# Cross network: the first layer's remainder products gathered at its end, and the last layer opened in column tiles

## The chip, the core and the metric

One core of a Trainium2 chip runs the whole computation. The core has five engines with instruction queues of their own: TensorE (PE, matrix products, with PEld for its weight loads), VectorE (DVE), ScalarE (ACT), GpSimd (POOL) and SyncE (SP, which here only issues DMAs). The metric is the device time of one launch in microseconds, smaller is better; the median of three runs stands for a kernel.

## The reference

A cross network of six layers. All arrays are bf16; B is 4096, D is 416 (26 x 16):

```python
def reference(x0, ws, bs):          # x0 [4096, 416], ws [6, 416, 416], bs [6, 416]
    x = x0
    for l in range(ws.shape[0]):
        x = x0 * (x @ ws[l] + bs[l]) + x
    return x
```

Each layer needs the whole previous one along D, but rows of the batch are independent of each other.

## The kernel before, in words

**Layout.** For the first five layers the data are transposed: D on the partitions, batch along the free dimension. 416 is 3 x 128 + 32, so there is a main part of three blocks (`XM`, index k or m) and a remainder of 32 rows (`XR`). The batch is cut into two halves `s` of 2048 columns, and each half into four column groups `g` of 512. The remainder's 32 rows of the four groups of one half are stacked on the 128 partitions of `XR`. Three buffers `XM[0..2]` and `XR[0..2]` hold x0 and, in turns, the layers' outputs. `XRd` holds x0's remainder once more, with its upper and lower 64 partitions exchanged, for the first layer's products of block m = 1.

**One tile of work.** For an output block m: products over k with `WM` (`full`, L212, in the first layer; `mm_full`, L179, with 32 output columns each and four side by side on the array, in the later ones), and products with the remainder rows `WR` (`row`, L219; `mm_row`, L185; 32 contraction rows each, four side by side). ScalarE adds the bias and moves the result from PSUM to SBUF (L163, `ew_main`), VectorE multiplies it by x0 (L164) and adds the layer's input (L167). The 32 remainder outputs are made by `mm_rem` (L191 with `WD`, a block-diagonal copy of the weights, and L196), and finished by `ew_rem` (L171 on ScalarE, L172 and L173 on VectorE).

**PSUM and t buffers.** All PSUM tiles come from one pool with four slots of two banks; a new tile waits until ScalarE has read the one that held its slot. ScalarE writes into six `t` buffers, which VectorE frees.

**First layer** (`first_layer(s)`, L206). For each half: the first two column groups of blocks 0 to 2 (`pa`), the remainder rows, then the other two groups (`pb`), their remainder rows, then `mm_rem` for this half. x0 arrives by transposed loads (`load_x0t`, eight, on SyncE's queue, one per half and group). x0's remainder arrives as 64-byte pieces: for the first half straight into `xrig` by four loads on ScalarE's queue (`load_xrem0`), for the second into `xrem` by one load on SyncE's queue, between two of the transposed ones (`load_xrem1`, L84), which GpSimd regroups into `xrig` (L132). `x0_rem(s)` turns `xrig` by four PE transposes (L155) into a PSUM tile, and VectorE copies it out three times (L158): once to `XR[0]`, twice, 64 partitions each, to `XRd`. For the second half this stands at the end of the first half's work: its four transposes follow the first half's `mm_rem`.

**Layers 1 to 4** (loop at L280). Six tiles (s, m) are worked off in pairs; n = 0, 2, 4 is the pair's first index. After the pair n = 0 comes `rem_pair` (L265), the remainder products of both halves. Layer 4's outputs go by transposed DMAs into `XLrows` (batch rows on the partitions).

**Last layer** (from L313). The roles are swapped: 128 columns of x are the weights and `WM` streams through, so that outputs have batch rows on the partitions. Eight quads of four 128-row tiles are worked off two quads at a time (`rounds`, L360). A round opens with `done` tiles through `mm_q_full` (L325), then the remainder rows and the bias (L331, L334, `mm_q_rem`), then the other tiles. ScalarE copies out (L352), VectorE multiplies by `X0rows` and adds `XLrows` (L353, L342), and a DMA writes the output.

**What sets the order.** A scheduler orders instructions on each engine by the program's order and its own estimate of when inputs are ready; `tc.keep_in_program_order` pins an instruction to the program's order on its engine. [...]

Of the kernel before, what the change touches and what calls it, by code (L numbers as in the profile page):

```python
# [9 lines left out]
ACT = mybir.ActivationFunctionType  # L10
ALU = mybir.AluOpType
BF16 = mybir.dt.bfloat16
# [4 lines left out]
def kernel(  # L17
# [43 lines left out]
    xrem = big.tile([P, 16, R], BF16)  # L61
    xrig = big.tile([P, NS, 4, P], BF16)
    XRd = big.tile([P, NS * CW], BF16)
# [9 lines left out]
    def load_x0t(s, g):  # L73
        c0 = col0(s, g)
        nc.sync.dma_start_transpose(out=XM[0][:, :, c0:c0 + CW], in_=x0[c0:c0 + CW, 0:NK * P])

    def load_xrem0():
        with nc.allow_non_contiguous_dma(reason="64B row segments"):
            for i in range(4):
                nc.scalar.dma_start(xrig[:, 0, i, :].rearrange("p (g r) -> p g r", g=NG), x0_v[:, i:16:4, NK * P:D])  # L80

    def load_xrem1():
        with nc.allow_non_contiguous_dma(reason="64B row segments"):
            nc.sync.dma_start(xrem[:], x0_v[:, 16:32, NK * P:D])  # L84

# [27 lines left out]
    load_x0t(1, 0)  # L113
    load_xrem1()
    for g in range(1, NG):
# [36 lines left out]

    def x0_rem(s, tpr):
        for i in range(4):
            nc.tensor.transpose(tpr[:, 128 * i:128 * i + 128], xrig[:, s, i, :], ident[:])  # L155
# [4 lines left out]
    def ew_main(l, s, m, h, pt, cur, nxt, pin=False):  # L160
        c0 = col0(s, 2 * h)
        t = tpool.tile([P, 2 * CW], BF16, name="t")
        nc.scalar.activation(t[:], pt[:].rearrange("p a b -> p (a b)"), ACT.Identity, bias=bM[:, m, l:l + 1], scale=1.0)  # L163
        prod = nc.vector.tensor_tensor(out=t[:], in0=t[:], in1=XM[0][:, m, c0:c0 + 2 * CW], op=ALU.mult)  # L164
        if pin:
            tc.keep_in_program_order(prod)
        nc.vector.tensor_tensor(out=nxt[:, m, c0:c0 + 2 * CW], in0=t[:], in1=cur[:, m, c0:c0 + 2 * CW], op=ALU.add)  # L167

    def ew_rem(l, s, pr, curR, nxtR):
        tr = tpool.tile([P, 2 * CW], BF16, name="t")  # L170
        nc.scalar.activation(tr[:, 0:CW], pr, ACT.Identity, bias=bR[:, l:l + 1], scale=1.0)  # L171
        nc.vector.tensor_tensor(out=tr[:, 0:CW], in0=tr[:, 0:CW], in1=XR[0][:, CW * s:CW * s + CW], op=ALU.mult)  # L172
        nc.vector.tensor_tensor(out=nxtR[:, CW * s:CW * s + CW], in0=tr[:, 0:CW], in1=curR[:, CW * s:CW * s + CW], op=ALU.add)  # L173

# [31 lines left out]
    def first_layer(s):  # L206
# [20 lines left out]
        if s == 0:  # L227
            for m in range(NK):
                full(pa[m], m, 0, 0, False)
            tp0 = psum.tile([P, CW], BF16, tag="ps", name="tpr")  # L230
            x0_rem(0, tp0[:])
# [11 lines left out]
        for m in range(NK):  # L243
            ew_main(0, s, m, 0, pa[m], cur, nxt)
        for m in range(NK):
# [34 lines left out]
    for l in range(1, LL):  # L280
# [12 lines left out]
        for n in range(0, len(tiles), 2):  # L293
# [12 lines left out]
            finish(tb)  # L306
            if n == 0:
                rem_pair(l, cur, curR, nxtR, feeds_last)
# [9 lines left out]
    def q_cols(q, g):  # L318
        s, i = quads[q]
        c = col0(s, g) + 128 * i  # L320
        return slice(c, c + 128)

    def mm_q_full(q, g, py, closes):
        for k in range(NK):
            nc.tensor.matmul(py[:, 0:D], lhsT=cur[:, k, q_cols(q, g)], rhs=WM[:, l, k, :],  # L325
                             start=((not closes) and k == 0), stop=(closes and k == NK - 1))
# [34 lines left out]
    for q, at, done in rounds:  # L361
# [49 lines left out]
```

## Time and profile before

| | us |
|---|---|
| median of three runs | 130.45 |
| lowest, highest | 130.38, 130.53 |
| the profiled execution | 130.58 |
| its span, first to last instruction | 128.8 |

| engine | busy, us | share of the span |
|---|---|---|
| PE | 123.6 | 96% |
| DVE | 106.7 | 83% |
| ACT | 86.9 | 67% |
| POOL | 6.2 | 5% |

By stage the span is cut so: the first layer up to about 26.8 us, layers 1 to 4 about 19.2 us each up to 103.7 us, the last layer from there on. TensorE's granted clock was 1.00 in every stage.

| window, us | PE busy | DVE busy | ACT busy | DMA share |
|---|---|---|---|---|
| 11.0 to 17.0 | 6.00 | 4.26 | 5.36 | 1.07 |
| 17.0 to 21.4 | 4.40 | 4.24 | 1.69 | 1.15 |
| 21.4 to 26.8 | 5.40 | 5.30 | 5.00 | 1.13 |
| 26.8 to 46.0 | 19.20 | 18.32 | 14.14 | 0.67 |
| 103.7 to 115.5 | 11.80 | 10.75 | 8.52 | 1.10 |
| 115.5 to 128.8 | 8.91 | 10.26 | 7.94 | 0.56 |

How to read it: busy time is the time in which an engine had an instruction under way; the DMA share is that of the core's 16 DMA engines and can pass 1 where packets overlap. A chain of waits is followed back from the last instruction, at each step to what released it; its lines are start, length, engine, tile and line number. In the timeline, "[0.29 <-ACT t L163]" says that the engine stood idle for 0.29 us before this instruction and that an instruction of ScalarE ended it.

### The profile page before, as it was taken

The page shows a single profiled execution, that of the slowest core. Times are in us where ns is not written, and L with a number is a line of the kernel's source. Part 1 is how long each engine was busy: PE and PEld are TensorE (multiplying, and loading weights), DVE is VectorE, ACT ScalarE, POOL GpSimd, SP SyncE. Part 2 cuts the span into 40 slices and gives each one's busy share as a digit, 9 for nine tenths or more (in the row PEclk, how much of TensorE's full clock was granted, in tenths as well). Part 3 has the DMA queues.
Part 4 walks back from the last instruction along what each step waited for, and adds up shares of the span by engine and source line. Part 5 has one row for each costly group of instructions (what it writes and reads, how often), then busy time and mean ns, then how long its engine had stood idle before and what let it go on. Part 6 is the DMA issues. An engine that isn't in the chain of part 4 may idle for free.

```text
span 128.8 us, 3973 instructions
## 1 busy us (share of the span) xinstructions
PE 123.6 (96%) x1691; PEld 55.1 (43%) x1691; DVE 106.7 (83%) x195; ACT 86.9 (67%) x99; POOL 6.2 (5%) x18
## 2 busy tenths in 40 slices
PE   7999999999999999999999999999999999999960
PEld 3343443344545444434444544444444445445420
DVE  0023989999999898989898989898989899898991
ACT  0138873887848667848668848668858896569670
POOL 4004300600000000000000000000000000000000
PEclk9999999999999999999999999999999999999999
DMA  4999999999990000000000000000297999985754
GB/s 95 244 231 207 163 153 264 253 328 333 336 291 9 5 0 8 0 0 5 0 5 0 5 0 5 0 5 0 45 163 169 119 237 191 217 261 186 235 178 138
DMA packets 42102, 16.37 MB, mean 127 GB/s; under 512 B 30906, under 2 KB 42084, under 8 KB 42084
## 3 DMA queue, kind: packets, MB, share of 16 engines
q1 hardware_dynamic: 39368, 15.53, 53.9%
q10 hardware_dynamic: 2716, 0.59, 2.5%
q8 instruction: 13, 0.21, 0.7%
q14 instruction: 5, 0.04, 0.1%
HBM read 6.15 MB, written 3.41 MB: 74 GB/s over the span
## 4 chain that ended last, share of the span: by engine, by line
PE 89%; DVE 6%; issue 2%; ACT 1%; DVEq 0%
PE pt L179 49%; PE ph L212 13%; PE py L325 8%; PE pt L185 5%; PE pr L196 5%; PE wps L139 4%; DVE t L353 4%; DVE o L342 2%; PE pr L191 2%; PE ph L219 1%; PE py L331 1%; PE py L334 1%; ACT t L352 1%; PE tpr L155 0%; PE pr L155 0%
## 5 line engine op out<-in xcount | busy, mean ns | idle before, releaser
L179 PE MATMUL pt<-XM,WM 128*32 128x512 bf16 x1152 | 65.2, 379 | 0.0
L163 ACT ACTIVATE t<-pt,bM 128x1024 bf16<-128x1024 f32 x48 | 49.6, 1115 | 18.5 <-PE pt L185 18.5
L164 DVE TENSOR_TENSOR t<-t,XM 128x1024 bf16<-128x1024 bf16 x60 | 41.4, 690 | 5.2 <-ACT t L163 5.2
L167 DVE TENSOR_TENSOR XM<-t,XM 128x1024 bf16<-128x1024 bf16 x60 | 41.8, 697 | 3.4
L179 PEld LDWEIGHTS <-WM 128*32 128x32 bf16 x1152 | 29.7, 97 | 33.8 <-issue 5.1
L352 ACT CAST t<-py 128x416 bf16<-128x416 f32 (+1 forms) x23 | 14.8, 642 | 4.8 <-PE py L325 2.6
L325 PE MATMUL py<-WM,XM 128*128 128x416 bf16 x96 | 17.7, 340 | 0.0
L212 PE MATMUL ph<-XM,WM 128*128 128x512 bf16 x72 | 16.5, 381 | 0.0
L163 ACT ACTIVATE t<-ph,bM 128x1024 bf16<-128x1024 f32 x12 | 12.5, 1114 | 3.4 <-PE ph L219 3.4
L325 PEld LDWEIGHTS <-XM 128*128 128x128 bf16 x96 | 9.0, 98 | 8.5 <-issue 1.4
L353 DVE TENSOR_TENSOR t<-t,X0rows 128x416 bf16<-128x416 bf16 (+1 forms) x23 | 10.4, 457 | 1.2 <-ACT t L352 1.2
L342 DVE TENSOR_TENSOR o<-t,XLrows 128x416 bf16<-128x416 bf16 (+1 forms) x23 | 10.4, 456 | 0.0
L212 PEld LDWEIGHTS <-WM 128*128 128x128 bf16 x72 | 6.7, 98 | 8.4 <-issue 1.1
L171 ACT ACTIVATE t<-pr,bR 128x512 bf16<-128x512 f32 x10 | 6.4, 685 | 2.7 <-PE pr L196 2.1
L196 PE MATMUL pr<-XM,WM 128*32 128x512 bf16 x120 | 8.2, 379 | 0.0
L185 PE MATMUL pt<-XR,WR 32*128 32x512 bf16 x96 | 7.3, 379 | 0.0
L139 PE MATMUL wps<-const-bfloat16-1.0 128*128 128x512 bf16 (+1 forms) x12 | 4.9, 592 | 0.8 <-PEq L395 0.8
L104 ACT ACT_TABLE_LOAD x1 | 1.3, 1283 | 6.0 <-DMA XM<-in_x_dram 6.0
L173 DVE TENSOR_TENSOR XR<-t,XR 128x512 bf16<-128x512 bf16 x10 | 4.2, 425 | 0.7
L196 PEld LDWEIGHTS <-WM 128*32 128x32 bf16 x120 | 3.2, 97 | 3.0
L150 DVE CAST bM<-pb 128x18 f32<-128x18 bf16 x1 | 0.2, 177 | 5.1 <-PE pb L149 5.1
L172 DVE TENSOR_TENSOR t<-t,XR 128x512 bf16<-128x512 bf16 x10 | 4.2, 420 | 0.0
(38 smaller groups left out, 33.5 us busy)
## 6 DMA issues: line engine op xcount, KB each, us to landing
X0rows<-in_x_dram SPq DMA_DIRECT2D x4, 832.0 KB, 11.5
out_dram<-o SPq DMA_DIRECT2D x9, 208.0 KB, 2.5
WM<-in_ws_dram SPq DMA_DIRECT2D x5, 312.0 KB
out_dram<-o SPq DMA_DIRECT2D x13, 104.0 KB, 1.9
WR<-in_ws_dram SPq DMA_DIRECT2D x4, 130.0 KB, 4.1
WM<-in_ws_dram ACTq DMA_DIRECT2D x1, 312.0 KB
XM<-in_x_dram SPq DMA_TRANSPOSE x8, 4.9
xrig<-in_x_dram ACTq DMA_DIRECT2D x4, 32.0 KB, 4.2
```

What stands on the lines that cost most here:

```text
L139: nc.tensor.matmul(wps[:, 0:cols], lhsT=warm[:, 0:P], rhs=warm[:, 0:cols], start=True, stop=True)
L163: nc.scalar.activation(t[:], pt[:].rearrange("p a b -> p (a b)"), ACT.Identity, bias=bM[:, m, l:l + 1], scale=1.0)
L164: prod = nc.vector.tensor_tensor(out=t[:], in0=t[:], in1=XM[0][:, m, c0:c0 + 2 * CW], op=ALU.mult)
L167: nc.vector.tensor_tensor(out=nxt[:, m, c0:c0 + 2 * CW], in0=t[:], in1=cur[:, m, c0:c0 + 2 * CW], op=ALU.add)
L179: nc.tensor.matmul(pts[g // 2][32 * q:32 * q + 32, g % 2, :], lhsT=WM[:, l, k, 128 * m + 32 * q:128 * m + 32 * q + 32], rhs=cur[:, k, c0:c ...
L185: nc.tensor.matmul(pts[g // 2][:, g % 2, :], lhsT=WR[32 * g:32 * g + 32, l, 128 * m:128 * m + 128], rhs=curR[32 * g:32 * g + 32, CW * s:CW ...
L196: nc.tensor.matmul(pr[32 * g:32 * g + 32, :], lhsT=WM[:, l, k, NK * P:D], rhs=cur[:, k, c0:c0 + CW], start=False, stop=(k == NK - 1), tile ...
L212: nc.tensor.matmul(pt[:, gl, :], lhsT=WM[:, 0, k, 128 * m:128 * m + 128], rhs=cur[:, k, c0:c0 + CW], start=(k == 0 and not after_row), sto ...
L325: nc.tensor.matmul(py[:, 0:D], lhsT=cur[:, k, q_cols(q, g)], rhs=WM[:, l, k, :], start=((not closes) and k == 0), stop=(closes and k == NK ...
L342: tc.keep_in_program_order(nc.vector.tensor_tensor(out=o, in0=t, in1=xl, op=ALU.add))
L352: nc.scalar.copy(tv, src)
L353: tc.keep_in_program_order(nc.vector.tensor_tensor(out=tv, in0=tv, in1=X0rows[:, b, :], op=ALU.mult))
```

## The change

Seven edits:

1. The second half's remainder of x0 is no longer turned by PE. Its load moves from SyncE's to ScalarE's queue, behind VectorE's copies of the first half's remainder (a one-column memset of `xrem` ties it to that place), and takes 16 consecutive batch rows to a partition. VectorE transposes it in blocks of 32 x 32 straight into `XR[0]`, and copies it twice into `XRd` from there.
2. GpSimd's regrouping copy goes; `xrig` shrinks to the first half.
3. The first half's `mm_rem` moves to the end of the second half, where both halves' remainder products follow each other. ScalarE's and VectorE's order there is written out: the first half's remainder sum, the three `pb` tiles, the second half's remainder sum.
4. The second half's first two column groups are worked off group by group instead of block by block.
5. In layer 1, `rem_pair` follows the pair n = 2 instead of n = 0.
6. The last layer's first two tiles are opened with products of 32 columns, four side by side, instead of full ones (`mm_q_open`).
7. `X0rows` is loaded in 12 pieces instead of 4.

```diff
-    xrig = big.tile([P, NS, 4, P], BF16)
+    xrig = big.tile([P, 4, P], BF16)
...
+    def pin(ins):
+        tc.keep_in_program_order(ins)
+
     def load_xrem0():
...
-                nc.scalar.dma_start(xrig[:, 0, i, :].rearrange("p (g r) -> p g r", g=NG), x0_v[:, i:16:4, NK * P:D])
+                nc.scalar.dma_start(xrig[:, i, :].rearrange("p (g r) -> p g r", g=NG), x0_v[:, i:16:4, NK * P:D])
 
     def load_xrem1():
+        pin(nc.vector.memset(xrem[:, 0, 0:1], 0.0))
         with nc.allow_non_contiguous_dma(reason="64B row segments"):
-            nc.sync.dma_start(xrem[:], x0_v[:, 16:32, NK * P:D])
+            pin(nc.scalar.dma_start(xrem[:], x0[SW:2 * SW, NK * P:D].rearrange("(p t) r -> p t r", p=P)))
...
     load_x0t(1, 0)
-    load_xrem1()
...
-    for q in range(4):
-        nc.sync.dma_start(X0rows[:, 8 * q:8 * q + 8, :], x0_v[:, 8 * q:8 * q + 8, :])
+    for q in range(12):
+        b0, b1 = NBT * q // 12, NBT * (q + 1) // 12
+        nc.sync.dma_start(X0rows[:, b0:b1, :], x0_v[:, b0:b1, :])
...
-    nc.gpsimd.tensor_copy(xrig[:, 1].rearrange("p i (g r) -> p i g r", g=NG), xrem[:].rearrange("p (g i) r -> p i g r", g=NG))
...
-    def x0_rem(s, tpr):
+    def x0_rem0(tpr):
         for i in range(4):
-            nc.tensor.transpose(tpr[:, 128 * i:128 * i + 128], xrig[:, s, i, :], ident[:])
+            nc.tensor.transpose(tpr[:, 128 * i:128 * i + 128], xrig[:, i, :], ident[:])
         for dst, src in ((slice(0, P), slice(0, P)), (slice(64, P), slice(0, 64)), (slice(0, 64), slice(64, P))):
             to = XR[0] if dst == src else XRd
-            nc.vector.tensor_copy(to[dst, CW * s:CW * s + CW], tpr[src])
...
+            pin(nc.vector.tensor_copy(to[dst, 0:CW], tpr[src]))
+        load_xrem1()
+
+    def x0_rem1():
+        pin(nc.vector.transpose(XR[0][:, CW:2 * CW].rearrange("p (j t) -> p t j", t=16), xrem[:]))
+        for dst, src in ((slice(64, P), slice(0, 64)), (slice(0, 64), slice(64, P))):
+            pin(nc.vector.tensor_copy(XRd[dst, CW:2 * CW], XR[0][src, CW:2 * CW]))
+
+    def ew_act(n, pt, bias):
+        t = tpool.tile([P, 2 * CW], BF16, name="t")
+        nc.scalar.activation(t[:, 0:n], pt, ACT.Identity, bias=bias, scale=1.0)
+        return t
...
         else:
-            for m in range(NK):
-                for gl in range(2):
+            for gl in range(2):
+                for m in range(NK):
                     full(pa[m], m, 0, gl, False)
...
         row(pb[1], 1, 1, False)
         row(pb[2], 2, 1, False)
+        if s == 0:
+            x0_rem1()
+            for m in range(NK):
+                ew_main(0, s, m, 1, pb[m], cur, nxt, pin_all=True)
+            return
         pr = psum.tile([P, 2, CW], FP32, tag="ps", name="pr")
-        mm_rem(0, s, pr[:, 0, :], cur, curR)
-        if s == 0:
-            x0_rem(1, pr[:, 1, :].bitcast(BF16)[:, 0:CW])
+        for r in range(NS):
+            mm_rem(0, r, pr[:, r, :], cur, curR)
+
+        def act_main(m):
+            return ew_act(2 * CW, pb[m][:].rearrange("p a b -> p (a b)"), bM[:, m, 0:1])
+
+        tb, tr = [act_main(0), act_main(1)], [ew_act(CW, pr[:, 0, :], bR[:, 0:1])]
+        tb.append(act_main(2))
+        tr.append(ew_act(CW, pr[:, 1, :], bR[:, 0:1]))
+        ew_rem(0, 0, None, curR, nxtR, True, tr[0])
         for m in range(NK):
-            ew_main(0, s, m, 1, pb[m], cur, nxt, pin=(s == 0))
-        ew_rem(0, s, pr[:, 0, :], curR, nxtR)
+            ew_main(0, s, m, 1, None, cur, nxt, True, tb[m])
+        ew_rem(0, 1, None, curR, nxtR, True, tr[1])
...
-            if n == 0:
+            if n == (2 if l == 1 else 0):
                 rem_pair(l, cur, curR, nxtR, feeds_last)
...
+    def mm_q_open(q, g, py):
+        c = q_cols(q, g).start
+        for k in range(NK):
+            for j in range(0, P, 32):
+                nc.tensor.matmul(py[j:j + 32, 0:D], lhsT=cur[:, k, c + j:c + j + 32], rhs=WM[:, l, k, :],
+                                 start=(k == 0), stop=False, tile_position=(0, j))
...
         for u in range(done):
-            mm_q_full(q, u, bank[u], False)
+            if q == 0:
+                mm_q_open(q, u, bank[u])
+            else:
+                mm_q_full(q, u, bank[u], False)
```

`ew_main` and `ew_rem` take a `t` that `ew_act` has already filled, and pin VectorE's multiplications (and in the second half its additions) to the program's order.

More of the change, by code (lines that the diff above doesn't have):

```diff
@@ L160, in ew_main @@
-    def ew_main(l, s, m, h, pt, cur, nxt, pin=False):
+            pin(nc.vector.tensor_copy(to[dst, 0:CW], tpr[src]))
[8 more added lines that the diff above has]
+        return t
@@ L161, in ew_main @@
+    def ew_main(l, s, m, h, pt, cur, nxt, pin_all=False, t=None):
         c0 = col0(s, 2 * h)
-        t = tpool.tile([P, 2 * CW], BF16, name="t")
-        nc.scalar.activation(t[:], pt[:].rearrange("p a b -> p (a b)"), ACT.Identity, bias=bM[:, m, l:l + 1], scale=1.0)
+        if t is None:
+            t = ew_act(2 * CW, pt[:].rearrange("p a b -> p (a b)"), bM[:, m, l:l + 1])
         prod = nc.vector.tensor_tensor(out=t[:], in0=t[:], in1=XM[0][:, m, c0:c0 + 2 * CW], op=ALU.mult)
-        if pin:
-            tc.keep_in_program_order(prod)
@@ L167, in ew_main @@
[L167 to L173, printed above, removed]
+        if pin_all:
+            pin(prod)
@@ new lines, in ew_main, with ew_rem @@
+        total = nc.vector.tensor_tensor(out=nxt[:, m, c0:c0 + 2 * CW], in0=t[:], in1=cur[:, m, c0:c0 + 2 * CW], op=ALU.add)
+        if pin_all and s:
+            pin(total)
+    def ew_rem(l, s, pr, curR, nxtR, pin_all=False, t=None):
+        tr = ew_act(CW, pr, bR[:, l:l + 1]) if t is None else t
+        prod = nc.vector.tensor_tensor(out=tr[:, 0:CW], in0=tr[:, 0:CW], in1=XR[0][:, CW * s:CW * s + CW], op=ALU.mult)
+        if pin_all:
+            pin(prod)
+        total = nc.vector.tensor_tensor(out=nxtR[:, CW * s:CW * s + CW], in0=tr[:, 0:CW], in1=curR[:, CW * s:CW * s + CW], op=ALU.add)
+        if pin_all:
+            pin(total)
@@ L230, in first_layer @@
             tp0 = psum.tile([P, CW], BF16, tag="ps", name="tpr")
-            x0_rem(0, tp0[:])
+            x0_rem0(tp0[:])
             for m in range(NK):
@@ L243, in first_layer @@
         for m in range(NK):
-            ew_main(0, s, m, 0, pa[m], cur, nxt)
+            ew_main(0, s, m, 0, pa[m], cur, nxt, pin_all=(s == 1))
         for m in range(NK):
```

## The prediction

> **What bounds the kernel now.** I read the page's busy shares first, then the chain of waits in order of time, then the timeline around the first layer and at the end.
>
> ```profile
> span 128.8 us, 3973 instructions
> PE 123.6 (96%) x1691; PEld 55.1 (43%) x1691; DVE 106.7 (83%) x195; ACT 86.9 (67%) x99; POOL 6.2 (5%) x18
> ...
> 15.41 0.33 PE ph L219 x4
> 15.73 0.33 PE pr L191 x4
> 16.06 0.65 PE pr L196 x12
> 16.71 0.33 PE pr L155 x4
> 17.04 3.88 PE ph L212 x18
> 20.93 0.54 PE ph L219 x8
> 21.47 3.99 PE ph L212 x18
> 25.46 0.33 PE ph L219 x4
> ...
> 32.60 0.21 PE pr L191 x4
> ...
> 103.71 1.16 PE py L325 x6
> 104.87 0.29 PE py L331 x4
> 105.16 0.18 PE py L334 x4
> 105.34 0.18 PE py L331 x4
> ```
>
> The columns are start, length, engine, tile, line. From 0.77 to 115.65 us the chain never leaves PE: each piece starts where the last ended. So a microsecond saved on PE before 115.65 is a microsecond at the end, if nothing else is late. Every change of array shape is visible too: four L191 products cost 0.33 after row-tiled work (L219) and 0.21 after work of their own kind; four L331 cost 0.29 after L325 and 0.18 after L334; 18 L212 cost 3.99 after rows and 3.88 after the transposes. A change of shape costs 0.11.
>
> After 115.65 VectorE sets the end, so its starting points matter:
>
> ```profile
> 101.97 0.69 DVE L164 TENSOR_TENSOR t<-t,XM 128x1024 bf16<-128x1024 bf16 x1 [0.29 <-ACT t L163]
> 111.41 0.59 DVE L353 TENSOR_TENSOR t<-t,X0rows 128x832 bf16<-128x832 bf16 x1 [0.38 <-ACT t L352]
> 116.55 0.59 DVE L353 TENSOR_TENSOR t<-t,X0rows 128x832 bf16<-128x832 bf16 x1 [0.42 <-ACT t L352]
> ```
>
> The bracket is the idle time before the instruction. VectorE had caught up at each of these points and stood waiting for ScalarE, which waited for PE; from 116.55 to 126.2 it runs almost without a gap. So its last run starts when PE delivers, as long as VectorE itself comes 0.42 early.
>
> **The change, part by part.**
>
> *First half's end (PE).* Before, rows, remainder products and transposes of the second half's remainder stand between 15.73 and 17.04, then 18 products: 0.33 + 0.65 + 0.33 + 3.88 = 5.19. After, the 18 products follow the rows directly: 3.99. The 16 remainder products move to the second half's end, directly behind the 16 there, with no change of shape: 0.22 + 0.65 = 0.87. Sum: 5.19 - 3.99 - 0.87 = **0.33 saved** (four transposes 0.22, one change of shape 0.11). The second half starts 1.31 earlier (15.73 for 17.04), its rows about 1.2 earlier (19.73), and layer 1 0.33 earlier (26.44).
>
> *Last layer's opening (PE).* Six 128x416 products, 1.16, become 24 of 32 columns, four side by side. Layer 4 ends in that same shape (L179), so the change of shape at 103.71 goes; that behind it, to L331, stays. No row shows 32-column products with 416 moving columns. Ends: 48 L179 take 2.59, 54 ns each; 24 at that pace would be 1.30, a loss of 0.14. If they run with the moving columns, six groups at the 1.05 left of 1.16 without the 0.11, a gain of **0.11**. I take the gain: L334 sends four products of 416 columns, each with its own weights, through in 0.18, or 45 ns each, so the 54 ns of L179 come from its 512 columns (216 for four).
>
> *VectorE in the first layer.* Removed: three copies from PSUM (0.42 and 0.86 for two) and the wait of 0.48 ahead of them. Added: a memset (0.06, like the one of dz), a transpose of 128x512 in blocks, two copies of 64x512. Nothing shows the transpose: from below the copy of that shape, 0.42; from above GpSimd's regrouping of the same elements (L132), 1.06. I take 0.5, nearer the row of the same engine, and 0.86 for the copies. They start behind the third L167 (ended 16.60) and end near 18.0, at the worst 18.6. PE's rows need them at 19.73, so 1.1 to 1.7 cover it; without that cover PE would stall by what is late beyond it.
>
> VectorE later: the first half's remainder sum is pinned ahead of the second half's last three tiles. It needs ScalarE's pass over `pr`, which can start at about 25.8 (24.59 + 0.33 + 0.65 and a pipeline) and takes 0.69; VectorE is done with the tiles before it near 25.8, so it stands for about 0.7. PE needs that sum in layer 1's rows at 29.0; it is written near 27.3. VectorE starts layer 1 some 0.4 later than before. Layer 1 has the room: its idle before 44.27 is 0.43 and before 50.10 another 0.43. The second remainder sum ends near 32.4; the pair of remainder products that reads it goes from 32.2 to about 37.6, which is why that move (in layer 1 alone, same shape on both sides, no cost) must come with the other.
>
> *ScalarE.* Its queue now issues the load of `xrem`, behind the two L108 copies (9.66 to 10.76). The four issues of xrig took 0.37 to 0.66 and SyncE's of xrem 0.58. Queued behind it is the first L163, which began at 11.09: it slips by about 0.3. Who waits: PE's second tile of the half's end at 12.82, for the accumulator that this L163 frees at 12.20. Cover 0.6; 0.3 is left. Nothing on the path; an issue of 1.0 would cost 0.3.
>
> *SyncE.* The xrem issue leaves its queue, where 0.64 passed from 10.31 to the next transposed load at 10.95; the last three such loads start that much earlier. The `X0rows` load in 12 pieces instead of 4 (7.84 of issuing before) is hidden: first use at 107.4, and SyncE's next work is near 90. GpSimd loses one copy of 1.06, off the path.
>
> *Loads of the second half.* PE reads its four column groups in order at 15.84, 17.78, 20.38 and 21.03 now. The trace's completion events have them at 13.53, 16.96, 19.81 and 21.16 before the change. With 0.64 off the queue the last lands near 20.5: 0.5 to spare. Bounds: its issue at 15.72 - 0.64 = 15.08, plus the shortest and longest issue-to-landing of these loads, 4.6 and 6.4: 19.7 to 21.5, a stall of 0 to 0.45.
>
> The row on which this leans: from 13.6 to 14.3 the 16 DMA engines were 27% busy, so the queue, not the engines, was short. The Trainium skill says the other thing (Trainium Kernel Development and Optimization, Key Constraints): queues of different engines share the 16 DMA engines, and a second issuer saves issue time alone. By it the xrem traffic would still stand in the way, the last load would land at 21.16, and the sum would be 0.13 smaller. In the first 6 us, where the engines were full, the trace agrees with it; in that gap it does not.
>
> **Sum.** 0.33 + 0.11 = 0.44. The profiled execution took 130.58, of which 128.8 is the span: 128.4 and 130.14 after. The median of the three runs is 130.45, 0.13 below that execution: **130.0 us**. The VectorE points move with it: 101.97 by 0.29 (all its idle), 111.41 and 116.55 by 0.44, since behind 101.97 it runs to 111.03, then 110.74, and PE's delivery (111.41 - 0.44 = 110.97) is later than that.
>
> **The rivals.**
>
> Loads late but little (12%). The last column group lands 21.2 to 21.5, stall 0.15 to 0.45: 130.15 to 130.45. For: 64-byte pieces next to transposed loads. Against: the empty stretch.
>
> The other side (10%): the load of xrem on ScalarE's queue takes turns with the transposed loads instead of standing between two of them. The second load of XM, issued at 2.17 beside the 64-byte pieces of xrig from ScalarE, took 6.4 to land, the others 4.6 to 4.9: 1.5 to 1.8 more. If the load behind 10.31 suffers so and the next two queue behind it, the last lands at 21.16 - 0.64 + 1.5 to 1.8 = 22.0 to 22.3, PE stands for 1.0 to 1.3 at 21.03, and with 0.44 won the time is **131.0 to 131.3**. It is a loss from a landing after 21.47 on. Against: WM's 312 KB were on the engines as well in those first microseconds.
>
> Weight loads exposed (4%): four 32-column loads take 0.11 by L191's rows, 27 ns each. If these of the opening did not run under the products, 24 x 27 = 0.65, 1.70 for 1.16, less 0.33: 130.45 + 0.21 = 130.66. Against: 48 L179 take exactly their columns. The Trainium skill has that rule (TensorE: Matmul & The Clock Gate, Part 3): a weight load overlaps running products only if its row group differs, and here all four share one. L179, with the same sharing, does not show it.
>
> Opening paced at 54 ns, or no gain there (8%): 130.26, or 130.12.
>
> VectorE's 0.7 of standing is not made up (6%): the gain ends at 116.55, 130.45. Against: its idle in layers 1 to 4.
>
> That the moves don't take place: the compiled order of the changed kernel has the 32 remainder products in one row, the 24 products in the opening and the pinned VectorE order, so I give it nothing.
>
> **How the numbers follow.** The forecast has 60%, own range 129.9 to 130.15. About 0.2% (0.26 us, below 130.19) is what a measurement of this kernel tells from no change. Faster: 0.60, plus 0.05 of the opening's rival and 0.05 of the late loads: 0.70. Same: 0.03 + 0.07 + 0.06 = 0.16. Slower: 0.10 + 0.04 = 0.14. The range 129.85 to 130.5 takes in the bounds of opening and loads and leaves out those 14%.
>
> **What would show it.** Between 15.4 and 26.8 the chain should hold no pr between the halves, L212's successor should start near 15.73, two groups of 0.33 and 0.22 for the remainder near 24.6, and layer 1 near 26.4. The opening should show 24 products in about 1.05. A gap on PE near 21.0 released by a DMA would be the loads; one near 12.8 released by ScalarE the late first pass; one near 19.7 released by VectorE the transpose. VectorE should still show idle time ahead of its run at about 116.1. If PE ends 0.44 earlier and the time does not move, I was wrong about the tail.

## The result and the profile after

The changed kernel takes 130.09 us (median of 21 runs, 129.98 to 131.13), the kernel before in the same measurement 130.52 (21 runs, 130.38 to 130.99). The ratio is 0.9977 with a 95% interval of 0.9966 to 0.9988: faster by 0.23%. The ratio goes by means, into which some high times enter (see below): the means differ by 0.30 us, the medians by 0.43. The profiled execution took 130.08, its span is 128.3 (128.8 before). Three executions of all that were measured ran at a granted clock of 0.76 to 0.85 and took 146.86 to 163.10, one of experiment 6 and two of the kernel before; they are left out of the ratios.

The first two lines are the page's head and its first busy row; the others are the chain of waits (start, length, engine, tile, line).

```profile
span 128.3 us, 4010 instructions
PE 122.8 (96%) x1705; PEld 55.3 (43%) x1705; DVE 108.0 (84%) x196; ACT 86.8 (68%) x99; POOL 5.7 (4%) x17
```

```profile
15.37 0.33 PE ph L238 x4
15.70 3.99 PE ph L231 x18
19.69 0.54 PE ph L238 x8
20.24 3.99 PE ph L231 x18
24.23 0.33 PE ph L238 x4
24.55 0.33 PE pr L210 x4
24.88 0.65 PE pr L215 x12
25.53 0.22 PE pr L210 x4
25.75 0.65 PE pr L215 x12
26.39 2.59 PE pt L198 x48
...
103.34 1.05 PE py L358 x24
104.40 0.29 PE py L369 x4
104.68 0.18 PE py L372 x4
```

Nothing stands between the halves at 15.70 any more. Of the remainder's two groups the first pays the change of shape (0.33) and the second does not (0.22). Layer 1 starts at 26.39, before at 26.77, and the last layer at 103.34, before at 103.71. Its opening takes 1.05 where it took 1.16. That is 0.37 + 0.11, and the span is 0.5 shorter. Of the 0.37, 0.04 lies ahead of the change: the rows at 15.37 began at 15.41 before.

VectorE's timeline in the first layer is where the profile looks different from what was forecast:

```profile
16.23 2.35 DVE L165 STREAM_TRANSPOSE XR<-xrem 128x512 bf16<-128x512 bf16 x1
18.62 0.61 DVE L167 COPY XRd<-XR 64x512 bf16<-64x512 bf16 x2
19.26 0.69 DVE L178 TENSOR_TENSOR t<-t,XM 128x1024 bf16<-128x1024 bf16 x1
...
26.87 0.69 DVE L181 TENSOR_TENSOR XM<-t,XM 128x1024 bf16<-128x1024 bf16 x1
27.48 0.42 DVE L187 TENSOR_TENSOR t<-t,XR 128x512 bf16<-128x512 bf16 x1
...
33.53 0.68 DVE L181 TENSOR_TENSOR XM<-t,XM 128x1024 bf16<-128x1024 bf16 x1
...
101.61 0.69 DVE L178 TENSOR_TENSOR t<-t,XM 128x1024 bf16<-128x1024 bf16 x1 [0.29 <-ACT t L171]
...
110.93 0.59 DVE L391 TENSOR_TENSOR t<-t,X0rows 128x832 bf16<-128x832 bf16 x1 [0.27 <-ACT t L390]
...
116.08 0.59 DVE L391 TENSOR_TENSOR t<-t,X0rows 128x832 bf16<-128x832 bf16 x1 [0.43 <-ACT t L390]
```

The block transpose takes 2.35 us, and the copies end at 19.23. PE's first product with `XRd` starts at 19.86 and the rows that hold it at 19.62, so 0.4 to 0.6 us were left. No bracket stands before 27.48: VectorE has no idle time there. It starts layer 1's additions at 33.53, 1.34 later than before:

```profile
32.19 0.69 DVE L167 TENSOR_TENSOR XM<-t,XM 128x1024 bf16<-128x1024 bf16 x1
```

At the three late points its idle times are back, and the points have moved by 0.36, 0.48 and 0.47.

The 21 times are not spread evenly: 15 lie at 129.98 to 130.20, six at 130.44 to 131.13. In the times of before, two of 21 lie that far (0.46 or more) above the fastest, a third 0.44. The experiments bear on this too.

### The profile page after: what moved, and what is told of

The parts are those of the page before. It is cut to its first block, busy times and chain, and to the rows that moved or that the text cites. A ratio compares the mean times of both kernels' runs of the same rounds, so it can differ in the third digit from the quotient of the medians.

```text
span 128.3 us, 4010 instructions
## 1 busy us (share of the span) xinstructions
PE 122.8 (96%) x1705; PEld 55.3 (43%) x1705; DVE 108.0 (84%) x196; ACT 86.8 (68%) x99; POOL 5.7 (4%) x17
## 4 chain that ended last, share of the span: by engine, by line
PE 81%; DVE 7%; DMA 6%; ACTq 2%; issue 1%; ACT 1%; DVEq 0%
PE pt L198 50%; PE ph L231 11%; PE pt L204 5%; PE pr L215 5%; DVE t L391 4%; PE py L363 4%; DMA xrig<-in_x_dram 4%; DVE o L380 3%; DMA out_dram<-o 2%; PE pr L210 2%; PE ph L238 1%; PE py L358 1%; ACTq L83 1%; PE py L369 1%; ACT t L390 1%
## 5 line engine op out<-in xcount | busy, mean ns | idle before, releaser
L363 PE MATMUL py<-WM,XM 128*128 128x416 bf16 x90 | 16.5, 339 | 0.0
L363 PEld LDWEIGHTS <-XM 128*128 128x128 bf16 x90 | 8.5, 98 | 7.8 <-issue 1.4
L133 POOL COPY WD<-WR 32x32 bf16<-32x32 bf16 (+1 forms) x8 | 3.6, 454 | 12.4 <-DMA WR<-in_ws_dram 12.0
```

## The experiments

Each is the changed kernel with one thing undone, moved or doubled. Ratios are to the kernel before, measured beside it; the changed kernel's is 0.9977.

**1. The opening as before (edit 6 undone).**

```diff
-            if q == 0:
-                mm_q_open(q, u, bank[u])
-            else:
-                mm_q_full(q, u, bank[u], False)
+            mm_q_full(q, u, bank[u], False)
```

> The changed kernel with the last layer's first two tiles opened by full products again (edit 6 undone). Theory (a change of array shape costs 0.11 on PE and the opening's products themselves cost the same): opening 1.16 instead of 1.05, all later PE pieces 0.11 later, span 128.4 and time 0.11 above the changed kernel's. Rival (the tail hides what the opening saves, because VectorE sets the end): same span as the changed kernel, 128.3, although PE is 0.11 later at the last round.

Median 130.36 (12 runs, 130.13 to 131.04), ratio 0.9989 [0.9975, 1.0002]. The opening takes 1.16 again, and the ratios differ by 0.0012, 0.15 us, with intervals that overlap: the size fits the 0.11. Its profiled execution took 131.03 and shows something else. The chain of waits:

```profile
15.65 5.97 DMA XM<-in_x_dram
21.63 0.04 issue
21.67 0.38 PE ph L231
...
27.23 2.59 PE pt L198 x48
```

The last transposed load landed at 21.63, PE stood for it, and layer 1 began at 27.23, 0.84 later than in the changed kernel's profile. The load's 16 completion events show 15 at 19.97 or earlier, the last at 21.63: one of them was 1.66 later than the others (each event is taken here as one DMA engine's share of the load).

**2. The pair of remainder products early again (edit 5 undone).**

```diff
-            if n == (2 if l == 1 else 0):
+            if n == 0:
```

> The changed kernel with layer 1's pair of remainder products back behind the first pair of tiles (edit 5 undone). Theory (edit 5 is what keeps PE from waiting for VectorE's second remainder sum, which the changed kernel writes at about 33.6): PE reaches the second half's remainder products at 33.1 and stands there for about 0.5 us, time 0.4 to 0.6 above the changed kernel's, no gain left over the kernel before. Rival (that sum would come early enough, edit 5 is for nothing): same time as the changed kernel within 0.1.

Median 131.07 (6 runs), ratio 1.0038 [1.0023, 1.0052]. PE's timeline has the wait where it was expected:

```profile
32.53 0.82 PE L215 MATMUL pr<-XM,WM 128*32 128x512 bf16 x12
33.92 0.40 PE L210 MATMUL pr<-XR,WD 128*32 128x512 bf16 x4 [0.57 <-DVE XR L190]
```

The twelve products take 0.65 when others follow, so the next group was due at 33.18: it starts 0.74 late, 0.57 of it idle by the bracket. The ratios differ by 0.0061, 0.8 us, more than the 0.4 to 0.6 that was expected. The profiled execution is 1.03 above the changed kernel's; the other 0.27 is `WR`, the first layer's remainder weights, which landed at 9.87 instead of 9.60 (experiment 12 shows why that counts). Edit 5 takes nothing off by itself; it moves the pair behind a VectorE that is late.

**3. The second half's remainder loaded on SyncE's queue again.** The new layout and the VectorE transpose stay.

```diff
-        pin(nc.vector.memset(xrem[:, 0, 0:1], 0.0))
-            pin(nc.scalar.dma_start(xrem[:], x0[SW:2 * SW, NK * P:D].rearrange("(p t) r -> p t r", p=P)))
+            nc.sync.dma_start(xrem[:], x0[SW:2 * SW, NK * P:D].rearrange("(p t) r -> p t r", p=P))
...
     load_x0t(1, 0)
+    load_xrem1()
...
-        load_xrem1()
```

> The changed kernel with the load of xrem back on SyncE's queue between the transposed loads, its layout and VectorE's transpose kept. Theory (the queue was what delayed the second half's transposed loads, not the DMA engines): the last one lands at about 21.2 instead of 19.6, PE asks for it at 20.9, so it stands for 0.3 and the time is 0.2 to 0.4 above the changed kernel's. Rival (both queues share the same DMA engines, so the queue is indifferent): landing and time as in the changed kernel within 0.1.

Median 131.33 (5 runs, 131.26 to 131.45), ratio 1.0059 [1.0046, 1.0072]: 1.1 us above the changed kernel, and the largest effect of any single edit.

```profile
22.01 3.40 PE L230 MATMUL ph<-XM,WM 128*128 128x512 bf16 x14 [0.89 <-DMA XM<-in_x_dram]
```

By the completion events the last three transposed loads landed at 16.87, 18.80 and, for 15 of 16 engines, 20.27 (16.42, 18.01 and 19.54 in the changed kernel); the sixteenth came at 21.97. So the queue's order makes the load 0.73 later on 15 engines, a little more than the 0.64 that one issue took from this queue before. That alone would have cost nothing: PE asked for the load at about 20.95, after 20.27. All that PE waited for is the late sixteenth, and with 0.13 from a later `WR` (9.73) it makes up the 1.19 by which layer 1 starts later (27.58). The forecast of 0.2 to 0.4 missed. As all five executions lie within 0.2 of each other, they probably all had the late engine; only one was profiled, and why this order brings it is not shown.

**4. The transpose with contiguous writes** (the second half's remainder columns in another order than the main part's).

```diff
-XR[0][:, CW:2 * CW].rearrange("p (j t) -> p t j", t=16)
+XR[0][:, CW:2 * CW].rearrange("p (t j) -> p t j", t=16)
```

> The changed kernel with VectorE's transpose writing its 16 blocks one behind the other instead of 32 bytes apart; the second half's remainder then has its batch columns in another order, so that part of the output is another one. Theory (the 2.35 us of the transpose come from its scattered writes): 0.6 to 0.8 us for the transpose, VectorE 1.6 earlier up to the middle of layer 1, standing then for 0.7 ahead of the first remainder sum, and the same time as the changed kernel within 0.1, since PE waits for none of it. Rival 1 (a block transpose costs 2.35 whatever it writes): 2.3 again. Rival 2 (VectorE's lateness does cost time at the end): 0.2 to 0.4 faster than the changed kernel.

Median 130.15 (12 runs), ratio 0.9979 [0.9959, 0.9999]: the changed kernel's time. VectorE's timeline:

```profile
16.29 0.71 DVE L165 STREAM_TRANSPOSE XR<-xrem 128x512 bf16<-128x512 bf16 x1
...
27.20 0.43 DVE L187 TENSOR_TENSOR t<-t,XR 128x512 bf16<-128x512 bf16 x1 [1.34 <-ACT t L171]
```

The same instruction with the same shape takes 0.71 when neighbouring elements are written side by side, and 2.35 when they are written 16 elements (32 bytes) apart. The 1.64 saved turn up as 1.34 of idle time ahead of the remainder sum, and the time does not move.

**5. The transpose twice.**

```diff
+        pin(nc.vector.transpose(XR[0][:, CW:2 * CW].rearrange("p (j t) -> p t j", t=16), xrem[:]))
```

> The changed kernel with VectorE's block transpose done twice in a row. Theory (the transpose is hidden only by the 0.4 to 0.6 us between VectorE's copies to XRd, done at 19.23, and PE's first product with them at 19.86): XRd is ready at about 21.6, PE stands there for 1.7 us, and the time is 1.5 to 1.9 above the changed kernel's. Rival (some microseconds more of VectorE in the first layer disappear, as VectorE has idle time in every layer): within 0.3 of the changed kernel.

One execution: 132.14 beside 130.51 of before. PE waits where the cover ends:

```profile
21.18 0.61 PE L239 MATMUL ph<-XR,WR 32*128 32x512 bf16 x6 [1.46 <-DVE XR L166]
```

2.33 more on VectorE make PE stand for 1.46 and the time 2.05 longer than the changed kernel's 130.09, a little more than the 1.5 to 1.9 expected: PE stands once more, for 0.31 at layer 1's rows (30.95), until VectorE has written the first remainder sum. The cover is real and short, and there is no room for a second use of it.

**6. Block order in the second half (edit 4 undone).**

```diff
-            for gl in range(2):
-                for m in range(NK):
+            for m in range(NK):
+                for gl in range(2):
```

> The changed kernel with the second half's first two column groups worked off block by block again (edit 4 undone). Theory (edit 4 only puts off the second group's first use, from 16.5 to 17.8, and its load lands at 16.4): 0 to 0.15 above the changed kernel where the loads are on time, more where they are late, so a wider scatter. Rival (edit 4 has no part in the gain): same median and scatter as the changed kernel.

Median 130.60 (11 runs, 130.05 to 130.99), ratio 0.9997 [0.9979, 1.0015]. PE's timeline in the profiled execution (130.99):

```profile
16.93 3.40 PE L231 MATMUL ph<-XM,WM 128*128 128x512 bf16 x15 [0.42 <-DMA XM<-in_x_dram]
```

With the blocks outermost, PE asks for the second column group after three products, at 16.3; it landed at 16.89. The last load was late as well (21.65, 15 of 16 at 19.98). The best executions come within 0.07 of the changed kernel's, measured apart, so edit 4 seems to buy no time of its own: it buys 1.3 us of slack for the second group.

**7. A third round of the last layer in pairs.** VectorE then has four instructions fewer (192 instead of 196).

```diff
-rounds = [(0, PAIRS, 2), (2, PAIRS, 2), (4, TURNS, 2), (6, ENDS, 1)]
+rounds = [(0, PAIRS, 2), (2, PAIRS, 2), (4, PAIRS, 2), (6, ENDS, 1)]
...
-            if at is not PAIRS:
+            if at is not PAIRS or (q == 4 and u >= 6):
```

> The changed kernel with the third round of the last layer closed in three pairs and two single tiles instead of one pair and six singles. Theory (from 116 us on VectorE sets the end; two tiles as a pair cost it 0.50 + 0.50, as singles 4 x 0.285 = 1.14, by the starts in the trace, and two more pairs are made): VectorE's last run ends 0.2 to 0.28 earlier, time 0.15 to 0.28 below the changed kernel's. Rival (a pair comes later than its first single would, so VectorE stands idle for what it saves): within 0.1 of the changed kernel.

Median 131.26 (12 runs), ratio 1.0065 [1.0039, 1.0091]: slower, the theory falls, and so does the rival's "within 0.1". A pair is ready only when its second tile is, so VectorE waits twice more:

```profile
116.48 0.58 DVE L380 TENSOR_TENSOR o<-t,XLrows 128x832 bf16<-128x832 bf16 x1
117.49 0.59 DVE L391 TENSOR_TENSOR t<-t,X0rows 128x832 bf16<-128x832 bf16 x1 [0.42 <-ACT t L390]
...
122.00 0.38 DVE L391 TENSOR_TENSOR t<-t,X0rows 128x416 bf16<-128x416 bf16 x1 [0.43 <-ACT t L390]
```

The second wait comes from PE. In the chain of waits PE stands for accumulators that ScalarE empties later: the last 21 products begin at 120.72 (120.06 in the changed kernel), although PE entered layer 1 0.10 earlier here (26.29), and VectorE's last run begins when their results come.

**8. The first half's remainder products back at its end (that part of edit 3 undone).** The second half's remainder is still turned by VectorE.

```diff
         if s == 0:
+            pr = psum.tile([P, 2, CW], FP32, tag="ps", name="pr")
+            mm_rem(0, 0, pr[:, 0, :], cur, curR)
             x0_rem1()
...
+            ew_rem(0, 0, pr[:, 0, :], curR, nxtR, True)
             return
...
-        for r in range(NS):
-            mm_rem(0, r, pr[:, r, :], cur, curR)
+        mm_rem(0, 1, pr[:, 1, :], cur, curR)
...
```

> The changed kernel with the first half's remainder products, sum and all, back at the end of the first half (half of edit 3 undone), the second half's remainder still turned by VectorE. Theory (gathering both halves' remainder products saves one change of shape, and starts the second half 0.98 earlier, which is what makes the last transposed load late in some executions): PE reaches layer 1 0.11 later than the changed kernel, the undisturbed time is 0.11 above it, and no execution is more than 0.4 above the fastest. Rival (the scatter of the changed kernel has nothing to do with the loads): the same share of executions 0.5 or more above the fastest as in the changed kernel.

Median 130.22 (12 runs, 130.08 to 130.59, eleven within 130.31), ratio 0.9976 [0.9965, 0.9987]. The second change of shape is visible in the chain of waits, each group of four at 0.33 (the view ends at 28 us):

```profile
15.74 0.33 PE pr L210 x4
16.08 0.65 PE pr L215 x12
...
25.57 0.33 PE pr L210 x4
25.91 0.65 PE pr L215 x12
26.55 1.50 PE pt L198 x25
```

Layer 1 starts 0.16 later (26.55), 0.05 of it from `WR` (9.65), the fastest execution is 0.10 slower, and the spread is narrower. That fits PE asking for the last load 1.0 later, at about 21.9. The ratio is the same: what gathering the products wins in an undisturbed execution, its smaller slack for the last load seems to give back in the others.

**9 and 10. TensorE's instruction fetch moved.** The changed kernel's trace shows 13 transfers of 16 KB of the kind "instruction", each one packet of 0.9 to 1.3 us; TensorE has 1705 products and as many weight loads, one transfer per 262 of them. In the profiles so far the first such fetch had started at 19.30 to 19.50 in the four in which one engine of the last load was late (experiments 1, 3, 5, 6), and at 17.44 to 19.21 in the others.

```diff
# experiment 9
-    pe_filler(9, CW)
+    pe_filler(7, CW)
+    pe_filler(18, 64)
# experiment 10
-    pe_filler(2, 2 * P)
-    pe_filler(9, CW)
+    pe_filler(8, CW)
```

> The changed kernel with two of the nine warming products ahead of the first layer replaced by 18 products of 64 columns: about the same TensorE time, 16 more warming instructions. Theory: where the last transposed load lands late in some executions (21.6 to 22.0 in the profiles of four earlier kernels), it is because a 16 KB fetch of TensorE's instructions takes one DMA engine for about 1.1 us at 19.3 to 19.5, while that load is under way; the fetch comes at a place in TensorE's instruction stream, so more instructions ahead bring it forward, to 16.8 to 18.5, where it can only hold up a load with slack. Then the last load lands whole by 20.3, TensorE has no wait for it, and no execution lies more than 0.4 us above the fastest; median 129.9 to 130.2, ratio near 0.997. Rival, the spread has another cause: the same share of executions (some 6 in 21) more than 0.35 us above the fastest, wherever the fetch lies.

> The changed kernel with 8 warming products in place of 11. By the theory that a fetch of TensorE's instructions makes the last transposed load late, fewer instructions ahead put the fetch off by the time of three products, to 19.3 or later, where four earlier kernels had it and their last load landed at 21.6 to 22.0: so more of the executions 0.4 to 1.0 us above the fastest than in the changed kernel, median 130.2 to 130.8, TensorE waiting for the last load in the profile. Rival, the spread has another cause: the changed kernel's median of 130.1 and its spread.

Experiment 9: median 130.23 (12 runs, 129.95 to 131.13), ratio 0.9977 [0.9963, 0.9991]. The fetch went to 16.46, and the last load landed whole, at 20.44 to 20.61, without a wait of PE. But three of 12 runs lie 0.39 or more above the fastest, one of them 1.18: the spread is not gone, so the theory is not borne out as an account of the spread. The profiled execution, 130.34, is itself one of the three: its `WR` landed at 9.85, 0.25 later than in the changed kernel's profile, and that is nearly its whole distance.

Experiment 10: median 130.47 (12 runs, 130.03 to 131.11), ratio 0.9999 [0.9980, 1.0018]. The times spread as expected, for another reason. The fetch came at 22.17, behind the last load, which landed at 19.15, the earliest of all. PE's timeline of this kernel shows what was lost instead:

```profile
0.77 4.00 PE L142 MATMUL wps<-const-bfloat16-1.0 128*128 128x512 bf16 x9 [0.77 <-PEq L435]
...
5.69 3.95 PE L230 MATMUL ph<-XM,WM 128*128 128x512 bf16 x9 [0.56 <-DMA XM<-in_x_dram]
```

The same view of the changed kernel:

```profile
0.77 4.50 PE L142 MATMUL wps<-const-bfloat16-1.0 128*128 128x256 bf16 x12 [0.77 <-PEq L436]
...
5.64 2.10 PE L231 MATMUL ph<-XM,WM 128*128 128x512 bf16 x9
```

The first nine products on x0 took 3.95 instead of 2.10: with three warming products fewer and 0.56 of standing still before the data, TensorE ran at half pace until 9.5, although the granted clock of these windows reads 1.00. The starts of its products lie 0.43 apart there and 0.21 to 0.22 later. Layer 1 starts at 27.36, 0.97 later than in the changed kernel, which is the 0.98 between the two profiled executions. The Trainium skill (TensorE: Matmul & The Clock Gate, Part 1) says so: half the rate until about 3.4 us of sustained work, by a window that runs on its own, so that the moment differs between runs. The traces agree that the moment differs, but not with a fixed 3.4 us: counted from the first product, at 0.77, the pace doubled after about 2.7 us in experiment 5's profile, after about 4 in the changed kernel's and after about 5.6 in experiment 1's; here 4.00 us of warming products did not bring it, and it came 3.8 after the products began again. Four of the 12 runs at 130.03 to 130.07 would fit a moment that differs.

**11. `X0rows` in 4 pieces (edit 7 undone).**

```diff
-    for q in range(12):
-        b0, b1 = NBT * q // 12, NBT * (q + 1) // 12
+    for q in range(4):
+        b0, b1 = NBT * q // 4, NBT * (q + 1) // 4
```

> The changed kernel with the plain copy of x0 loaded in 4 pieces as before, not 12. Theory: the pieces land by 36 and are first used near 107, so the median is the changed kernel's within 0.1 us (130.0 to 130.2, ratio near 0.997). Rival: the number of pieces counts, through DMA engines that they share with the loads of the first layer or through their issues on SyncE: 0.2 us or more to either side.

The rival holds, and by more than it asked for: median 130.60 (12 runs, 130.43 to 131.66), ratio 1.0021 [1.0002, 1.0041]. With this edit undone the whole change gains nothing. Even the fastest execution is 0.45 above the changed kernel's fastest, measured apart. The profile is of one of the longer executions (131.66): its last load was late by one engine (22.11, 15 of 16 at 20.34; fetch at 19.78), and the last output landed 1.98 us after its issue began, where the changed kernel has 1.73. Between layer 1's start and the last addition nothing differs by more than 0.02. So of the 0.45 the profile shows 0.25, at the very end. The 4 pieces alone do not bring that: the kernel before has them too, and its last output landed after 1.75, as in every other profile (1.72 to 1.75). `WR` landed 0.11 later as well (9.71), a delay that the late load hid in this execution; whether the others had it is not shown.

**12. Four pieces, and 8 small loads behind them.**

```diff
+    spare = big.tile([P, 16], BF16)
...
-    for q in range(12):
-        b0, b1 = NBT * q // 12, NBT * (q + 1) // 12
+    for q in range(4):
+        b0, b1 = NBT * q // 4, NBT * (q + 1) // 4
         nc.sync.dma_start(X0rows[:, b0:b1, :], x0_v[:, b0:b1, :])
+    for q in range(8):
+        nc.sync.dma_start(spare[q:q + 1, :], bs[0:1, 0:16])
```

> The plain copy of x0 in 4 pieces, and behind them on SyncE's queue 8 loads of 32 bytes into a spare tile, so that this queue has as many issues as in the changed kernel. With 4 pieces alone every execution was at 130.43 or above, where the changed kernel's fastest 15 of 21 lie at 129.98 to 130.20. Theory A, the count of issues on SyncE's queue decides (where in its stream the instruction fetches fall, and so which transfer at the end they hold up: in the run with 4 pieces the last write landed 1.99 us after its issue began, in the changed kernel 1.74): the fastest executions are back at 130.0 to 130.2 and the last write lands within 1.8. Theory B, the size of the pieces decides (832 KB in one transfer): the fastest executions stay at 130.4 or above.

Median 129.81 (11 runs, 129.66 to 130.78), ratio 0.9949 [0.9929, 0.9969]: the fastest version of all, ahead of the kernel before by 0.5% and of the changed kernel by about 0.3 us, measured apart. Theory B falls: the same large pieces come with the fastest times. The end is as A expected (last output 1.73 after its issue began), but the time is lower than A gave, so A is not borne out as it stands either. The timelines of PE and ScalarE show where that comes from. This kernel:

```profile
9.33 0.54 ACT L113 COPY WR<-WR 32x416 bf16<-32x416 bf16 x1 [1.70 <-DMA WR<-in_ws_dram]
9.89 0.54 ACT L113 COPY WR<-WR 32x416 bf16<-32x416 bf16 x1
...
10.48 0.60 PE L241 MATMUL ph<-XR,WR 32*128 32x512 bf16 x6
10.71 0.38 PE L241 MATMUL ph<-XRd,WR 32*128 32x512 bf16 x2
```

The changed kernel, the same views:

```profile
9.63 0.54 ACT L112 COPY WR<-WR 32x416 bf16<-32x416 bf16 x1 [2.05 <-DMA WR<-in_ws_dram]
10.19 0.54 ACT L112 COPY WR<-WR 32x416 bf16<-32x416 bf16 x1
...
10.62 0.60 PE L238 MATMUL ph<-XR,WR 32*128 32x512 bf16 x6
11.01 0.38 PE L238 MATMUL ph<-XRd,WR 32*128 32x512 bf16 x2
```

The last row products of the first half need the copy of the remainder weights that ScalarE makes second. It ends at 10.73 in the changed kernel (10.19 + 0.54), and they start 0.28 later; here it ends at 10.43, and they start 0.28 later again. So the first layer's first rows hang on the small load of `WR`, which landed at 9.60 there and at 9.30 here. In the chain of waits that stands only as eight row products of 0.69 instead of 0.54, and so it does in the kernel before: a wait of 0.15 that no bracket names. The 18 products behind start 0.30 earlier (11.02 for 11.32), which is the whole difference at the end (spans 128.0 and 128.3). In 13 of the 14 profiles these 18 products start 1.71 to 1.72 after `WR` has landed, and it lands at 9.30 to 9.87; the exception is experiment 10, whose TensorE was at half pace. So this load sets PE's time in the first layer, and its landing alone can move a run by 0.57, more than the change gains. Counted from the first packet of `xrig`, the load ahead of it on ScalarE's queue, `WR` is there after 4.5 us here and after 4.7 to 5.1 in the other profiles. Why is open: this kernel differs in its issues on SyncE's queue and in a 32-byte tile that shifts the addresses of `xrig` and of what follows it, and no run takes the two apart. The issues come too late to delay or speed this load themselves: the first that differs is at about 24 us, and `WR` is there at 9.30.

## Why the prediction came out

**TensorE's 0.33 and 0.11: right.** Layer 1 starts 0.38 earlier, 0.34 of it from the change and 0.04 from a `WR` that landed at 9.60 instead of 9.64; the opening is 0.11 shorter. The groups and their lengths are those forecast, at most 0.05 off in place. Experiments 1 and 8 put the two changes of shape back, and they show as 0.11 each in the profiles; in the measured times 0.11 is less than the intervals. The weight loads of the opening stay under the products: with all four sharing a row group, 24 products took 1.05. So the rule of the Trainium skill quoted in the prediction (TensorE: Matmul & The Clock Gate, Part 3) does not hold in this case.

**"The chain never leaves PE" from 0.77 on: not the whole of it.** Up to about 11.35 PE's time hangs on the load of `WR`, in the kernel before as well, by the 1.71 of experiment 12. The forecast does not suffer, because what it saves lies behind that point.

**VectorE's transpose: mis-sized.** "I take 0.5", with an upper bound of 1.06; it took 2.35, over twice the upper bound. The bounds came from copies that write side by side, and with such writes this one takes 0.71, inside them (experiment 4). The cover of "1.1 to 1.7" was 0.4 to 0.6. Nothing reached the path, as forecast, but with a third of the margin; experiment 5 shows that the next 2.3 us do.

**VectorE's 0.7 of standing: not there.** The 2.35 used it up. VectorE entered layer 1 1.34 late, not 0.4. The rest of the argument held: the remainder sum was written at 28.35 (forecast 27.3), ahead of layer 1's rows at 28.92, and the idle times of layers 1 to 4 took in the delay. They took in more than was reckoned: the point at 101.97 moved by 0.36 and still has 0.29 of idle time ahead of it. Experiment 4, with 1.34 of idle time before the remainder sum, has the same time.

**ScalarE's slip of 0.3: not there.** The issue of `xrem` (0.62 at 10.00) ran beside the second copy, and the first pass over `ph` began at 11.05 (11.09 before).

**The loads: right in the profile, wrong as a certainty.** The last landed at 19.64, before the forecast 20.5 and just outside its bounds of 19.7 to 21.5. The forecast spoke of one landing time; the runs show two kinds of execution, and where one engine is late PE loses about 0.75 or more. The rival "loads late but little", at 12%, comes nearest to what experiments 1 and 6 show, but their load landed at 21.6, later than its 21.5, and cost more than its 0.45. Some of the six high times among 21 may be of this kind; none of the six was profiled. The rival on the other side had the queues the wrong way round: on ScalarE's queue the load harms nothing that shows, on SyncE's the time is 1.1 longer, nearly all of it a late engine (experiment 3). By the Trainium skill (Trainium Kernel Development and Optimization, Key Constraints) a second issuer saves issue time alone. The prediction made of that a last load at 21.16 as before, which does not follow, since the rule grants the issue time. The load landed at 19.64, 1.52 earlier; with `xrem` back on SyncE 15 of 16 engines were done at 20.27. The 0.63 to 0.73 that the queue is worth is about the 0.64 of one issue, so the traces do not go against the rule. The other 0.89 was there with `xrem` on SyncE's queue too, and no run takes it apart.

**`X0rows` in 12 pieces: costed at nothing, and wrong.** "Hidden" is true of the issuing, for nothing waits for the pieces. Yet with 4 pieces the gain is gone (experiment 11), and with 4 pieces and the same count of issues it is there again (experiment 12). So an edit that moves no work on the path is worth as much as the change itself. Whether it acts by the count of issues or by where instructions and buffers lie is not shown. The forecast hit the time by accounting for the work that moved, and it would have missed by 0.45 for the same kernel with 4 pieces, without anything in its reasoning to warn of it. That part of the prediction was luck.

**What stays open.** Why one engine of the last load is late in some executions: in all five such profiles an instruction fetch began at 19.30 to 19.78, while that load was under way; of the nine others eight have it outside that span, and experiment 12's, at 19.74, began when the load had landed, at 19.48. But counted from the load itself the two kinds do not differ. In the five the fetch began 0.49 to 0.80 before the other 15 engines were done. In four of the nine (the changed kernel, experiments 2, 4 and 7) it began 0.72 to 0.75 before, and there the sixteenth was only 0.10 to 0.11 behind. So a fetch under way is not enough, and with the high times left in experiment 9 it can be at most one cause. Also open are 0.1 to 0.2 of experiment 11's 0.45, its late end, and the quicker load of `WR` in experiment 12.

## What to carry to other kernels

Find in the chain what one change of array shape costs and gather work of one shape: 0.11 of PE's time here, each time. What is gathered can take slack from something else, here from the last load (experiment 8). When an operation that the trace does not show is bounded by copies of the same shape, ask first how far apart its writes lie, and look for the work that covers it at several times the estimate. Look for a load that no bracket names: a constant distance between its landing and the work behind it, in profile after profile, gives it away. At differences of 0.3% an edit that moves no work can weigh as much as the work that is moved: try a version with a neutral change before crediting or blaming an edit.

## What the runs showed of the hardware that was not expected

- VectorE's block transpose of 128x512 takes 0.71 us with contiguous writes and 2.35 with writes 32 bytes apart.
- A fetch of 16 KB of instructions is one packet of 0.9 to 1.3 us in the changed kernel's trace. In nine profiles one began 0.5 to 0.8 us before most of the last transposed load had landed; in five of them one of the load's 16 completions came 1.66 to 1.77 us after the other 15, in four 0.10 to 0.11 after.
- The landing of one small load, 26 KB of weights, differed from profile to profile between 9.30 and 9.87, and the work behind it followed 1.71 to 1.72 after.
- With three warming products fewer, one of 512 columns and two of 256, and 0.56 of standing still, the next nine products took 3.95 instead of 2.10 in the profiled execution.
- Eight loads of 32 bytes that nobody reads, with a tile of 32 bytes per partition, came with a kernel about 0.3 us faster than the changed one and 0.8 us faster than the one with the same four pieces and without them.
